# Sparse attention and a feed-forward block on one core: the products with the end keys in 64x32 tiles

## The chip, the cores and the metric

The kernel runs on one core of a Trainium2 chip. The metric is the device time of one execution in microseconds (us); the median of three runs is compared. PE is TensorE's matmul side, PEld its weight loads, DVE is VectorE, ACT is ScalarE, POOL is GpSimd, SP is SyncE. TensorE's granted clock is given as a share of 2.4 GHz.

## What is computed

Attention over 4 batches of 8 heads, 768 positions and head size 64, followed by a feed-forward block on all 3072 tokens (512 to 2048 to 512). Only some blocks of 32 keys count for a block of 32 queries:

```python
scores = scale * np.matmul(q, k.transpose(0, 1, 3, 2))
mask = np.abs(blk_i - blk_j) <= window                    # window = 1
mask = mask | (blk_i == 0) | (blk_j == 0) | (blk_i == n_blocks - 1) | (blk_j == n_blocks - 1)
for qb in range(n_blocks):
    for kb in sampled_blocks[qb]:                         # three drawn blocks
        mask[qb * block:(qb + 1) * block, kb * block:(kb + 1) * block] = True
scores = np.where(mask, scores, -1000000000.0)
...
attn = attn / (np.sum(attn, axis=-1, keepdims=True) + 1e-09)
return np.matmul(attn, v).astype(np.float32)

h = x @ w_in
sp = np.maximum(h, 0.0) + np.log1p(np.exp(-np.abs(h)))
g = h * erf(sp)
return (g @ w_out).astype(np.float32)
```

So a block of queries inside the sequence looks at eight blocks of keys: the first and the last of the sequence (the end keys), three neighbours and three drawn ones. The first and the last block of queries look at all keys.

## The kernel before

Queries and keys lie with head size on the partitions, two heads of a pair on rows 0 to 63 and 64 to 127. Work on the scores comes in units. A unit of kind "m" is four blocks of queries (128 rows of scores) of two pairs of heads; there are 10 for each batch, 40 in all. A unit "e" is the last two inner blocks of two pairs (2 for each batch, 8 in all), a unit "f" is the two end blocks of queries of one pair against all keys (4 for each batch).

`scores` (L575) makes the products of a unit in fp32, in one PSUM tile `s` of two banks (one for each head of a pair). For "m" and "e" it runs over `turns`, the two pairs: first the end keys, 64 columns (`blocks_of(rows, pr, 0, NB, NB - 1)` takes the first and the last block), into columns 192 to 255 of each group, then the six near and drawn blocks, 192 columns, for each block `j` of queries apart. The end keys are the same for all blocks of queries, so one product has all of a unit's queries of a head as its stationary operand: 64 rows by 128 columns for "m" (four products), 64 by 64 for "e" (four products). The near products have 32 stationary columns, since each block of queries has its own keys: 64 by 32 tiles, 16 products for "m" and 8 for "e". An fp32 product appears in the trace as two MATMUL and two LDWEIGHTS instructions, a product of fp16 as one of each.

`soft_max`, `soft_exp` and `soft_low` (DVE and ACT) turn `s` into probabilities in two fp16 halves, `soft_turn` transposes them by a DMA of SP's queue (on PE for the first four units), and `values` (L623) multiplies them with the rows of values two units later: 96 fp16 products of 128 by 32 tiles and 64 or 65 columns into `po` for an ordinary place (192 LDWEIGHTS and MATMUL in all), and 192 products for the places of the "e" and "f" units.

The order is written out by hand; every instruction stays in program order on its engine. After a prologue (load, scale and split the weights, four units) a loop over 96 groups of the feed-forward block runs. One step of it issues on PE, in this order: `ff_first` (24 products of 256 columns into `h`), `values` of a unit begun two units earlier, `scores` of a new unit, `ff_second` of the group before the last (12 products of 512 columns into `o`). Steps without a unit have `h` and `o` alone. The table `until` says how many units have begun by which group. `s` is one buffer, so that `scores` waits until ACT has read the unit before.

Of the kernel before, what the change touches and what calls it, by code (L numbers as in the profile page):

```python
# [19 lines left out]
BLOCK = 32  # L20
# [22 lines left out]
def sparse_attention_moe(ctx: ExitStack, tc: tile.TileContext, qT, kT, v, sampled, w_in, w_out, out):  # L43
# [22 lines left out]
    pe, act, dve, pool, sp = (InOrder(e) for e in (nc.tensor, nc.scalar, nc.vector, nc.gpsimd, nc.sync))  # L66
    B, H, D, S = qT.shape
    NB = S // BLOCK
# [38 lines left out]
    def key_blocks(b):  # L107
        return keys[:, b % 2 * (NB + 1) : (b % 2 + 1) * (NB + 1)]
# [456 lines left out]
    def near_keys(b, i, rows, pr):  # L565

        c = slice(pr * BLOCK, (pr + 1) * BLOCK)
        first = b % 2 * (NB + 1) + i - 1
        near = keys[rows, first : first + NR, c]
        apart = (kgs[b, i] - first) * HP * BLOCK  # L570
        return bass.AP(near.tensor, near.offset, [near.ap[0], (apart, 2), near.ap[1], near.ap[2]])
# [3 lines left out]
    def scores(unit):  # L575
        kind, b, n = unit[0], unit[1], unit[2:]
        tag = "_".join(str(x) for x in unit)
        s = ps_s.tile([P, 1024], F32, tag="s", name=f"s_{tag}")
        q = qts[b, n[0] if kind == "m" else MT]
        both = [slice(a * D, (a + 1) * D) for a in range(2)]  # L580

        def blocks_of(rows, pr, start, stop, step=1):
            return key_blocks(b)[rows, start:stop:step, pr * BLOCK : (pr + 1) * BLOCK]

        if kind == "f":
            (pr,) = n
            for c, e in ((0, 512), (512, S)):
                for rows in both:
                    k = blocks_of(rows, pr, c // BLOCK, e // BLOCK)
                    pe.matmul(s[rows, c:e], q[rows, pr, 2 * BLOCK :], k, start=True, stop=True)  # L590
            softs[unit] = (s[:, :S], 1, S)
            return
        if kind == "m":
            t, quad = n
            s4 = s.rearrange("p (a r w) -> p a r w", a=2, r=2)
            first, count, turns = 1 + 4 * t, 4, [(r, 0, s4[:, :, r]) for r in range(2)]
            softs[unit] = (s, 4, 256)
        else:
            (quad,) = n
            s3 = s.rearrange("p (a w) -> p a w", a=2)[:, :, :256]  # L600
            first, count, turns = NB - 3, 2, [(r, r * D, s3) for r in range(2)]
            softs[unit] = (s3, 2, 256)
        for r, o, out in turns:
            pr = 2 * quad + r
            for a, rows in enumerate(both):
                k = blocks_of(rows, pr, 0, NB, NB - 1)
                pe.matmul(
                    out[o : o + count * BLOCK, a, 192:], q[rows, pr, : count * BLOCK], k, start=True, stop=True
                )
        for r, o, out in turns:  # L610
            pr = 2 * quad + r
            for j in range(count):
                c = j * BLOCK
                for a, rows in enumerate(both):
                    place = out[o + c : o + c + BLOCK, a, :192]
                    near = near_keys(b, first + j, rows, pr)
                    pe.matmul(place, q[rows, pr, c : c + BLOCK], near, start=True, stop=True)
# [243 lines left out]
    def seen(unit):  # L861

        if unit[0] == "m":
            return unit[1:]
        if unit[0] == "f" and unit[2] % 2 == 1:
            return unit[1], MT, unit[2] // 2
        return None
# [48 lines left out]
    for quad in range(2):  # L916
        square_v(0, quad)
    scale_v(0)
    scores(units[0])
    split_v(0, 0, 0)  # L920
    split_v(0, 0, 1)
# [7 lines left out]
    have_v.add(0)  # L929

    scores(units[1])
    used_keys(units[1])
    gathers(0)
# [8 lines left out]

    soft_turn(units[1])
    scores(units[2])
    work("Di4 Qi4 Di5")
    soft_max(units[2])
# [43 lines left out]
    for m in range(len(groups) + FF_LAG):  # L990
# [12 lines left out]
        place = seen(old) if old and begun - PV_LAG >= FIRST else None  # L1003
# [82 lines left out]
```

## Time and profile before

| | us |
|---|---|
| median of 3 runs (826.76 to 829.26) | 828.74 |
| the profiled execution | 831.7 |
| its span on the core | 829.9 |
| PE busy | 698.5 |
| DVE busy | 570.1 |
| ACT busy | 551.3 |
| POOL busy | 126.8 |

The span is the time from the first to the last instruction of the profiled execution; 1.8 us of the profiled time lie around it. PE is busy for 84% of the span and the other engines for less. The first quarter is the prologue, in which PE is idle for half of the time; from then on it is busy nearly throughout. The timeline gives for each run of like instructions the start, the length, the engine, the tiles, the number of instructions, and in brackets the idle time ahead of it and what ended it. "Issue" there is a wait for nothing that the profile shows.

### The profile page before, as it was taken

How to read it: one execution, taken by the hardware profiler on the slowest of the kernel's cores; microseconds unless marked ns; L12 is line 12 of the kernel's file. 1: busy time of each engine (PE TensorE's matmuls, PEld its weight loads, DVE VectorE, ACT ScalarE, POOL GpSimd, SP SyncE). 2: the span in 40 equal slices, each digit the busy share in tenths (PEclk: the TensorE clock that was granted, in tenths of full speed). 3: DMA queues.
4: the chain of work that ended last, by engine and by line, in shares of the span. 5: the costliest groups of instructions: out<-in, count | busy, mean ns of one | idle time of the engine just before them, and what ended most of it. 6: DMA issues, size and time to landing. Idle time of an engine off the chain costs nothing. (4 is left out here: it accounts for less than half of the span.)

```text
span 829.9 us, 26567 instructions
## 1 busy us (share of the span) xinstructions
PE 698.5 (84%) x10844; PEld 460.2 (55%) x10844; DVE 570.1 (69%) x987; ACT 551.3 (66%) x943; POOL 126.8 (15%) x343
## 2 busy tenths in 40 slices
PE   1254546888986879999999988999999999999997
PEld 1133423555654647566666556666666665666664
DVE  3994696787865666885668766876677767754454
ACT  4654567987755656776668657767677676675774
POOL 4621131002222121100103231000111110000000
PEclk9999767999998999999999999999999999999999
DMA  8999963887799898773598898752688858220000
GB/s 306 289 267 295 250 164 66 164 182 196 176 197 199 215 207 185 162 167 47 134 206 193 171 223 201 177 96 45 162 192 175 182 103 184 44 53 16 1 26 26
DMA packets 199930, 131.59 MB, mean 159 GB/s; under 512 B 144000, under 2 KB 167168, under 8 KB 199808
## 3 DMA queue, kind: packets, MB, share of 16 engines
q1 hardware_dynamic: 196384, 118.10, 62.5%
q0 software_dynamic: 3424, 11.80, 4.4%
q8 instruction: 85, 1.39, 0.7%
q14 instruction: 37, 0.30, 0.1%
HBM read 83.88 MB, written 12.95 MB: 117 GB/s over the span
## 5 line engine op out<-in xcount | busy, mean ns | idle before, releaser
L59 PE MATMUL h<-xT,wi 128*128 128x256 f16 x2304 | 275.7, 277 | 17.0 <-ACT wi L59 9.3
L59 PE MATMUL o<-wo,g 128*128 128x512 f16 x1152 | 271.4, 385 | 10.1 <-issue 3.5
L59 PEld LDWEIGHTS <-wi 128*128 128x128 f16 x2304 | 227.9, 99 | 68.7 <-ACT wi L59 10.8
L59 PEld LDWEIGHTS <-g 128*128 128x128 f16 x1152 | 109.0, 99 | 150.9 <-issue 32.4
L59 ACT ACTIVATE x<-x 128x512 f32<-128x512 f32 x288 | 181.5, 630 | 9.1
L59 POOL COPY keys<-keys 128x128 f32 x264 | 92.4, 397 | 260.1 <-PE s_m L59 173.8
L59 DVE SCALAR_TENSOR_TENSOR q<-x,q 128x512 f32<-128x512 f32 x96 | 67.8, 706 | 65.4 <-ACT x L59 65.4
L59 ACT ACTIVATE x<-h,isg 128x512 f32<-128x512 f32 x96 | 65.5, 682 | 67.7 <-PE h L59 67.6
L59 ACT ACTIVATE pf_m<-s_m,nb_m 128x256 f32<-128x256 f32 x160 | 62.6, 473 | 57.1 <-DVE nb_m L59 54.2
L59 PE MATMUL s_m<-keys,qt 64*32 64x192 f32 (+1 forms) x1600 | 71.6, 344 | 12.5 <-issue 6.1
L59 ACT ACTIVATE q<-q 128x512 f32<-128x512 f32 x96 | 60.7, 633 | 32.0 <-DVE q L59 32.0
L59 DVE SCALAR_TENSOR_TENSOR q<-q,h 128x512 f32<-128x512 f32 x96 | 65.5, 683 | 22.6 <-ACT q L59 22.6
L59 DVE SCALAR_TENSOR_TENSOR g<-q,g 128x512 f16<-128x512 f32 x96 | 66.6, 694 | 3.3
L59 PE MATMUL po<-vb,pT_m 128*32 128x65 f16 (+1 forms) x3840 | 45.8, 203 | 26.9 <-DMA vb<-vtab 15.1
L59 ACT ACTIVATE q<-x 128x512 f32<-128x512 f32 x96 | 60.5, 630 | 3.0
L59 DVE TENSOR_REDUCE mx_m<-s_m 128x4 f32<-128x1024 f32 x40 | 48.8, 1219 | 19.3 <-PE s_m L59 19.0
L59 PEld LDWEIGHTS <-pT_m 128*32 128x32 f16 x3840 | 39.0, 99 | 38.5 <-DMA vb<-vtab 16.8
L59 PEld LDWEIGHTS s_m<-keys,qt 64*32 64x32 f32 (+1 forms) x1600 | 45.2, 130 | 26.4 <-issue 9.5
L59 DVE TENSOR_TENSOR p_m<-pf_m,p_m 128x1024 f16<-128x1024 f32 x40 | 49.1, 1227 | 3.2 <-ACT p_m L59 2.2
L59 DVE TENSOR_TENSOR x<-xf,x 128x512 f16<-128x512 f32 x24 | 17.6, 734 | 38.9 <-ACT x L59 38.9
L59 DVE TENSOR_SCALAR g<-q 128x512 f16<-128x512 f32 x96 | 41.6, 433 | 3.3
L59 POOL COPY keys<-wi 128x768 f32<-128x768 f32 (+1 forms) x24 | 16.3, 705 | 163.7 <-DMA wi<-in_kT_dram 163.7
(111 smaller groups left out, 523.4 us busy)
## 6 DMA issues: line engine op xcount, KB each, us to landing
vb<-vtab SPq DMA_DIRECT2D x280, 65.0 KB, 3.3
vb<-vtab SPq DMA_DIRECT2D x32, 390.0 KB, 5.0
vraw<-in_v_dram SPq DMA_DIRECT2D x10, 768.0 KB, 5.6
vtab<-vn SPq DMA_DIRECT2D x16, 390.0 KB, 5.6
vb<-vtab SPq DMA_DIRECT2D x12, 520.0 KB, 6.1
qt<-in_qT_dram SPq DMA_DIRECT2D x20, 256.0 KB, 3.5
out_dram<-wo SPq DMA_DIRECT2D x20, 256.0 KB, 5.4
vb<-vtab SPq DMA_DIRECT2D x36, 130.0 KB, 3.3
```

What stands on the lines that cost most here:

```text
L59: done = call(*args, **kwargs)
```

## The change

The end keys are multiplied for each block of queries apart, as the near keys are. For each pair the products now run over `j` and the two heads: 32 stationary columns in place of 128 ("m") or 64 ("e"), 64 moving columns as before, and the result goes to the same places. A unit "m" has 16 products with the end keys in place of 4, a unit "e" 8 in place of 4. Nothing else is changed.

```diff
@@ -602,11 +602,12 @@
             softs[unit] = (s3, 2, 256)
         for r, o, out in turns:
             pr = 2 * quad + r
-            for a, rows in enumerate(both):
-                k = blocks_of(rows, pr, 0, NB, NB - 1)
-                pe.matmul(
-                    out[o : o + count * BLOCK, a, 192:], q[rows, pr, : count * BLOCK], k, start=True, stop=True
-                )
+            for j in range(count):
+                c = j * BLOCK
+                for a, rows in enumerate(both):
+                    place = out[o + c : o + c + BLOCK, a, 192:]
+                    ends = blocks_of(rows, pr, 0, NB, NB - 1)
+                    pe.matmul(place, q[rows, pr, c : c + BLOCK], ends, start=True, stop=True)
         for r, o, out in turns:
             pr = 2 * quad + r
             for j in range(count):
```

On PE, with no other row changed there, the place of the unit of batch 3, turn 1, quad 0, between the last rows of `values` and the first of `ff_second`. Before:

```order
L59 MATMUL po_0_0_10169<-vb,pT_m_0_0_9784 32x65
L59 MATMUL s_m_1_0_10290<-keys,qt_1_9684 128x64 x4
L59 MATMUL s_m_1_0_10290<-keys,qt_1_9684 32x192 x16
L59 LDWEIGHTS g_1_2_10096
L59 MATMUL o_1_0_0_9824<-wo,g_1_2_10096 128x512
```

After:

```order
L59 MATMUL po_0_0_10577<-vb,pT_m_0_0_10180 32x65
L59 MATMUL s_m_1_0_10698<-keys,qt_1_10068 32x64 x16
L59 MATMUL s_m_1_0_10698<-keys,qt_1_10068 32x192 x16
L59 LDWEIGHTS g_1_2_10504
L59 MATMUL o_1_0_0_10220<-wo,g_1_2_10504 128x512
```

The four products with 128 stationary columns have become sixteen with 32, ahead of the sixteen near ones, and the rows around them stand where they stood. A product of fp32 is one row here with its weight load, so 16 of the trace's instructions have become 64.

The same on PE for the second "e" unit of batch 2, between the values of the end blocks and the feed-forward block. Before:

```order
L59 MATMUL po_5_0_9324<-vb,pT_f_1_9224 32x65
L59 MATMUL s_e_1_9517<-keys,qt_5_8190 64x64 x4
L59 MATMUL s_e_1_9517<-keys,qt_5_8190 32x192 x8
L59 LDWEIGHTS g_0_4_9264
L59 MATMUL o_0_0_0_9066<-wo,g_0_4_9264 128x512
```

After:

```order
L59 MATMUL po_5_0_9704<-vb,pT_f_1_9604 32x65
L59 MATMUL s_e_1_9897<-keys,qt_5_8542 32x64 x8
L59 MATMUL s_e_1_9897<-keys,qt_5_8542 32x192 x8
L59 LDWEIGHTS g_0_4_9644
L59 MATMUL o_0_0_0_9446<-wo,g_0_4_9644 128x512
```

Here four products with 64 stationary columns have become eight with 32, that is 16 of the trace's instructions have become 32.

## Rows read from the trace of the kernel before

**Rows 1.** The page: busy time with its share, and PE and its clock in 40 slices.
```profile
PE 698.5 (84%) x10844; PEld 460.2 (55%) x10844; DVE 570.1 (69%) x987; ACT 551.3 (66%) x943; POOL 126.8 (15%) x343
PE   1254546888986879999999988999999999999997
PEclk9999767999998999999999999999999999999999
```

**Rows 2.** Busy us and instructions by window: PE, PEld, DVE, ACT, POOL, clock, DMA, GB/s.
```profile
500.00:600.00 100.00, 96.80 (x1502) 62.75 (x1501) 72.33 (x131) 68.37 (x119) 9.42 (x31) 0.98 0.59 136
600.00:700.00 100.00, 97.78 (x1702) 66.60 (x1701) 75.62 (x136) 71.37 (x128) 12.31 (x42) 1.00 0.81 172
```

**Rows 3.** Timeline of PE, one step and a half: start, length, work, idle before.
```profile
642.06 1.47 PE L59 MATMUL s_m<-keys,qt 64*128 64x64 f32 x40
643.47 2.76 PE L59 MATMUL o<-wo,g 128*128 128x512 f16 x12
646.07 2.78 PE L59 MATMUL h<-xT,wi 128*128 128x256 f16 x24
648.78 0.96 PE L59 MATMUL po<-vb,pT_m 128*32 128x65 f16 x96
649.67 1.11 PE L59 MATMUL s_m<-keys,qt 64*128 64x64 f32 x15
651.17 0.86 PE L59 MATMUL s_m<-keys,qt 64*32 64x192 f32 x25 [0.39 <-issue]
```

**Rows 4.** Windows on the scores' tiles: end and near part ("m"), end part ("e").
```profile
331.28:331.87 0.59, 0.59 (x8) 0.52 (x8) 0.00 (x0) 0.00 (x0) 1.00 0.77 223
331.87:332.68 0.81, 0.81 (x34) 0.49 (x32) 0.00 (x0) 0.00 (x0) 1.00 0.37 39
...
553.94:554.22 0.28, 0.28 (x9) 0.21 (x9) 0.00 (x0) 0.00 (x0) 1.00 0.25 59
```

**Rows 5.** Groups by form, PE, all units "m": count, busy us, mean ns, idle before.
```profile
L59 PE MATMUL s_m<-keys,qt 64*32 64x192 f32 x1280 | 45.4, 354 | 5.9 <-issue 3.7 <-POOL keys L59 1.9 <-POOL vn L59 0.2
...
L59 PE MATMUL s_m<-keys,qt 64*128 64x64 f32 x320 | 29.0, 303 | 6.7 <-ACT pf_m L59 4.3 <-issue 2.4
```

**Rows 6.** Windows from one stall of PE's issue to the next, columns as in Rows 2.
```profile
206.09:231.71 25.62, 23.85 (x383) 14.95 (x383) 20.76 (x35) 19.18 (x34) 5.66 (x15) 0.93 0.74 156
231.71:252.53 20.82, 16.90 (x381) 11.61 (x380) 14.28 (x26) 10.29 (x21) 5.95 (x14) 1.00 0.97 222
...
305.80:376.61 70.81, 67.64 (x1019) 43.94 (x1020) 53.54 (x97) 51.08 (x89) 9.03 (x28) 0.98 0.82 177
...
651.16:758.86 107.69, 104.44 (x1531) 68.98 (x1530) 72.07 (x130) 74.11 (x124) 5.47 (x18) 1.00 0.46 95
```

**Rows 7.** Timeline of PE at two of these stalls.
```profile
252.53 1.25 PE L59 MATMUL s_m<-keys,qt 64*128 64x64 f32 x36 [2.39 <-issue]
...
588.11 0.88 PE L59 MATMUL s_m<-keys,qt 64*32 64x192 f32 x30 [0.82 <-issue]
```

**Rows 8.** DMA queues: packets, MB, share of 16 engines.
```profile
q8 instruction: 85, 1.39, 0.7%
```

**Rows 9.** Windows of 256 instructions that end at a stall, columns as in Rows 2.
```profile
373.43:376.61 3.18, 1.71 (x149) 1.59 (x142) 0.69 (x1) 3.05 (x5) 0.00 (x0) 1.00 1.22 99
...
584.65:588.11 3.45, 2.64 (x148) 2.14 (x133) 1.51 (x5) 2.57 (x5) 0.00 (x0) 1.00 0.26 67
755.10:758.86 3.76, 2.26 (x153) 1.71 (x139) 2.33 (x6) 2.88 (x6) 0.00 (x0) 1.00 0.01 4
```

**Rows 10.** Timeline of PE: long waits for other engines and transfers.
```profile
262.63 0.22 PE L59 MATMUL po<-vb,pT_m 128*32 128x65 f16 x1 [3.40 <-DMA vb<-vtab]
...
479.17 1.09 PE L59 MATMUL po<-vb,pT_m 128*32 128x65 f16 x96 [1.91 <-DMA pT_m<-p_m]
...
517.06 2.44 PE L59 MATMUL s_f<-keys,qt 64*64 64x512 f32 x8 [1.95 <-ACT pf_m L59]
...
692.52 1.10 PE L59 MATMUL po<-vb,pT_m 128*32 128x65 f16 x96 [1.69 <-DMA pT_m<-p_m]
```

## The prediction

> **What bounds the kernel now.** I read the page's busy lines first, then the windows, then the timeline of PE step by step. PE is the busiest engine, and from the second quarter on its slices stand at 8 and 9 tenths at the full clock [rows 1]. Late in the span it is busy for 97 to 98 us of each 100, DVE and ACT for 68 to 76 [rows 2]. The page's chain of waits ends after 3% of the span and decides nothing here. In the timeline a step runs `s`, `o`, `h`, `po`, `s` without a gap: 1.47, 2.76, 2.78 and 0.96 us [rows 3]. So in such a stretch what PE saves shortens the step.
>
> Two things break that. PE waits for transfers and for ACT in places: 3.40 us, 1.91 us, 1.95 us and 1.69 us are long ones [rows 10]. What PE saves just ahead of one of these mostly makes the wait longer. The last that does not hang on a place close by in PE's own work is at 517 us; the one at 692 us waits for a transposed unit that PE itself made earlier, so I let it move along.
>
> And PE stops where nothing holds it but "issue". Look at the counts between such stops: 383 + 383, 381 + 380, 1019 + 1020, 1531 + 1530 matmuls and weight loads [rows 6], that is 766, 761, 2039 and 3061, each a few short of 768, 768, 2048 and 3072. The few are semaphore instructions, which these counts leave out. So the stops stand at multiples of 256 instructions. The queue named "instruction" carried 85 packets of 1.39 MB in all [rows 8], 16.4 KB each; 10844 + 10844 instructions [rows 1] in 85 portions are 255 each. PE's instructions therefore come in blocks of 256, and PE stops when a block is not there yet. Two of these stops show 2.39 and 0.82 us of idle time [rows 7].
>
> How long a block takes can be read too: 256 instructions that end at a stop took 3.18, 3.45 and 3.76 us [rows 9], all in dense work that alone would be done in 1.5 to 2 us. I take 3.5 us from entering a block until the next one can be used. A block of `o` and `h` work is far longer: 48 instructions of `h` take 2.78 us and 24 of `o` 2.76 us [rows 3]. Only `po` and `s` run dense enough to outrun the supply: `po` has 192 instructions in 0.89 us, from 648.78 to 649.67 [rows 3], 4.6 ns each.
>
> **What the change saves on PE.** The end part of a unit "m" takes 0.59 us, the near part 0.81 us [rows 4]. In the end part eight weight loads of 128 columns fill 0.52 us [rows 4]; the loads set its pace. The changed end part has the form of the near one, with 64 moving columns in place of 192 and as many instructions (the near part: 1280 matmuls in 40 units [rows 5], 32 for each). By columns it takes a third of 0.81, 0.27 us; by the pace of `po`, 32 pairs of load and matmul at 9.3 ns, 0.30 us. The two ends are close, and the change of form between the parts goes away, which speaks for less. I take 0.27 and keep 0.20 to 0.30: 0.32 us saved (0.29 to 0.39). For "e" the end part takes 0.28 us [rows 4] and will have half the instructions of "m", 0.14: 0.14 saved. Were all of it to count, 40 x 0.32 + 8 x 0.14 = 13.9 us. Up to some 215 us PE is idle for much of the time [rows 1], so I count nothing there; up to 517 us the waits of rows 10 take most back. Behind 517 us stand ten units "m" and four "e": 10 x 0.32 + 4 x 0.14 = 3.8 us.
>
> The Trainium skill, "TensorE: Matmul & The Clock Gate", section "Wait — 56ns, not 53.3ns?", says that matmuls never start closer than about 25 ns. By it 32 of them would take 0.8 us, and the end part would be 0.2 us longer. The 4.6 ns for each instruction of `po` [rows 3] speaks against it.
>
> **What the change adds.** Each "m" gets 48 more instructions on PE and each "e" 16: 40 x 48 + 8 x 16 = 2048, eight more blocks. Ahead of a unit's scores stand 192 instructions of `po`; with the 80 of the scores they were 272 in some 2.0 us, now 320 in about 1.6 us. A block that begins in the first third of `po` now ends inside the scores; before, only one that began in the first 16 instructions did. I counted the changed order forward in blocks of 256, from the place that the stops of before give (a block begins 194 instructions behind PE's first), which I take as unchanged because nothing ahead of the first matmul changes. Worked in full: one block behind 517 us holds the last 166 of a `po`, the 64 of the end part and 25 near ones (and a semaphore); 166 x 4.6 ns + 0.13 (the gap between `po` and `s`) + 0.27 + 0.25 = 1.4 us against 3.5, a stop of 2.1 us. Price and contents of the others behind 517 us: 256 of the longer `po` of the end units twice (about 1.4 us: 2.1 each, or 1.5 where the block begins early in `po`, when PE's queue runs ahead), the same block as the worked one two units later (2.0), one of 120 `po`, 128 scores and 7 `o` (2.6 us: 0.9), one of 256 `po` that begins right behind `h` (0.5 to 2.1). That is six, 7.9 to 11.2 us; I take 9.3. Two more begin 20 instructions before the end of `h` and last 2.4 us; before, such a block cost 0.39 us of idle time in one place [rows 3], so 0 to 1.1 each, and I take none. The stop at 759 us ends a block that holds the same instructions before and after, and cancels.
>
> Taken away are the stops of before in this stretch. With the pace lost around them they cost 1.1 us at 588 us, 0.7 at 651 and about 0.5 elsewhere, 2.3 us [rows 3, 7]. Added: 9.3 - 2.3 = 7.0 us (5.6 to 11.1).
>
> Ahead of 517 us the same count gives about 3 us more of stops than before, and 6.6 us less of PE's work; both stand between long waits [rows 10], and I put them at nothing, between -4 and +3. No other engine's instructions change. What covers the rest: DVE and ACT have a quarter of each 100 us free [rows 2], so a step 0.3 us shorter leaves them time. More stops also give the other engines time, so some of the 7.0 is taken back from waits; I keep that in the range.
>
> Sum: 831.7 - 3.8 + 7.0 = 834.9 for the profiled execution, which stands 3.0 above the median; for the median 828.74 + 3.2, rounded 832.0.
>
> **The rivals.**
> 1. The blocks come in time, or their stops only fill waits that are there anyway, and the shorter scores count: 828.74 - 3.8 = 825; with all 30 "m" and 6 "e" behind 215 us, 10.4 us, 818. For it: most blocks of before came in time. Against: [rows 6, 7]. The Trainium skill, "Runtime: NRT & Kernel Launch", section "Instruction fetch mechanics", says that instructions come in blocks of 16 KiB, 256 of them, and that crossing into one is mostly hidden. By that rule the added instructions cost nothing, which is this rival; the block size agrees with the trace, the hiding does not.
> 2. Gain and stops cancel: half of the 7.0 us is taken back by waits, 828.74 - 3.8 + 3.5, about 828.5. For it: a stop of 2.39 us at 252 us [rows 7] stands ten us ahead of a wait for a transfer of 3.40 us [rows 10], which without the stop would have been longer.
> 3. All added stops are paid, those ahead of 517 us too, and the two uncertain ones: 828.74 - 3.8 + 11.1 + 2.2 = 838. It decides from the point at which transfers delay the blocks beyond 3.5 us.
> 4. Small products don't run at the pace of `po`: 0.2 us more for each of 40 units, 8 us: 837.
>
> **How the numbers follow.** The forecast, slower through missing instructions, has 0.50 (829.5 to 836; a fifth of it lies under 831.2), rival 1 0.24 (of this 0.05 near 818), rival 2 0.18, rival 3 0.05, rival 4 0.03. 0.3%, about what a measurement of this kernel can tell from no change, is 2.5 us. Faster by more: 0.22, from rival 1. Within: rival 2, a fifth of the forecast, and 0.04 from the edges of rival 1 and of the forecast, 0.32. Slower: what is left, 0.46. The range leaves out the far end of rival 1 and most of rival 3: 822 to 837. The likeliest case alone spans 829.5 to 836.
>
> **What would show it.** The end part of an undisturbed unit at about 0.27 us and no gap before the near part; 32 matmuls in its form; 93 packets on the instruction queue; stops of issue at multiples of 256 instructions, at least a dozen of them, several inside `s` right behind `po` and inside the long `po` of the end units. It would be wrong if the stops stand where they stood, or if fewer appear because the blocks begin elsewhere; then PE's step is simply shorter, and rival 1 holds.

## The result and the profile after

The changed kernel takes 838.42 us, the median of ten runs (833.09 to 840.43); the kernel before, run beside it ten times, 827.89 (825.23 to 834.43). The ratio over all runs is 1.0111, between 1.0081 and 1.0141: 9.2 us slower, 6.7 to 11.7 (the two medians alone lie 10.5 us apart). The forecast was 832.0 and the range ended at 837. The direction was right, the size was not.

The profiled execution took 838.55 us, its span 836.8. The page, with the lines that answer to [rows 1] and [rows 8]:

```profile
PE 694.4 (83%) x11868; PEld 455.9 (54%) x11868; DVE 567.9 (68%) x987; ACT 551.3 (66%) x943; POOL 128.9 (15%) x343
PE   1242735888987989998899898999899999999997
PEclk9995666999998999999999999999999999999999
q8 instruction: 93, 1.52, 0.8%
```

PE is busy for 4.1 us less than before and the span is 6.9 us longer, so PE stands idle for 11 us more. 1024 matmuls and 1024 weight loads are added, and eight packets of instructions, 93 in place of 85.

The timeline of PE at an undisturbed step (start, length, work, count, idle time before), to set beside [rows 3]:

```profile
637.08 0.96 PE L59 MATMUL po<-vb,pT_m 128*32 128x65 f16 x96
637.97 1.26 PE L59 MATMUL s_m<-keys,qt 64*32 64x64 f32 x64
639.16 2.76 PE L59 MATMUL o<-wo,g 128*128 128x512 f16 x12
641.76 2.78 PE L59 MATMUL h<-xT,wi 128*128 128x256 f16 x24
```

The scores take 1.26 us in place of 1.47. The end part alone, from the windows on the scores' tiles, for a unit "m" and a unit "e", to set beside [rows 4]:

```profile
399.80:400.07 0.27, 0.27 (x33) 0.27 (x33) 0.00 (x0) 0.00 (x0) 1.00 0.00 1
...
561.52:561.66 0.14, 0.14 (x17) 0.14 (x25) 0.00 (x0) 0.00 (x0) 1.00 0.00 0
```

0.27 and 0.14 us, as forecast. But the end part became 0.32 us shorter and the scores only 0.21: the near part now fills 1.26 - 0.27 = 0.99 us where 1.47 - 0.59 = 0.88 were left before.

The stops of PE's issue, windows from one to the next as in [rows 6], and two blocks of 256 that end at one as in [rows 9]:

```profile
594.93:604.30 9.37, 8.73 (x254) 6.06 (x255) 6.35 (x11) 4.94 (x10) 3.37 (x12) 1.00 0.66 153
604.30:619.82 15.52, 14.20 (x255) 9.44 (x255) 12.10 (x23) 10.38 (x19) 1.78 (x6) 1.00 0.87 184
...
591.62:594.93 3.31, 1.63 (x145) 1.50 (x137) 0.99 (x2) 2.81 (x5) 0.00 (x0) 1.00 0.26 70
615.87:619.82 3.95, 2.63 (x153) 1.77 (x137) 3.78 (x9) 3.42 (x6) 1.78 (x6) 1.00 1.01 236
```

509 and 510 instructions lie between these stops, a few short of 512, and the blocks take 3.3 and 4.0 us: the mechanism of the prediction. What it did to the time is read from the view of waits, cut by stretch: who waited for what, us in total, times, longest. First the kernel before, up to 215 us, from there to 570 us, and behind:

```profile
PE po L59 <- issue: 6.1, 3, 2.9
...
PE s_m L59 <- issue: 4.9, 3, 2.4
PE o L59 <- issue: 3.5, 2, 2.6
PE po L59 <- issue: 3.2, 2, 1.7
...
PE s_m L59 <- issue: 1.2, 2, 0.8
```

The kernel after, in the same three stretches:

```profile
PE po L59 <- issue: 8.5, 3, 4.9
...
PE s_m L59 <- issue: 15.6, 8, 2.9
PE po L59 <- issue: 3.8, 2, 3.0
PE o L59 <- issue: 1.1, 1, 1.1
PE s_e L59 <- issue: 0.2, 1, 0.2
...
PE po L59 <- issue: 1.7, 1, 1.7
PE o L59 <- issue: 1.3, 1, 1.3
PE s_m L59 <- issue: 1.2, 2, 0.6
```

6.1, 11.6 and 1.2 us became 8.5, 20.7 and 4.2: 14.5 us more, 33.4 in place of 18.9, and 11.5 of them stand ahead of 570 us, 10.5 of these ahead of 517 us, in the stretch that the prediction had put at nothing. Most wait in front of a piece of `s`, eight times in the middle stretch.

The stops are not all of it. `o`, unchanged in the code, on the page of the kernel before and of the kernel after (count, busy time, mean in ns, idle time before):

```profile
L59 PE MATMUL o<-wo,g 128*128 128x512 f16 x1152 | 271.4, 385 | 10.1 <-issue 3.5
L59 PE MATMUL o<-wo,g 128*128 128x512 f16 x1152 | 277.1, 391 | 8.0 <-issue 2.5
```

`o` takes 5.7 us more. As PE's busy time as a whole fell by 4.1 us, its other work takes 9.8 us less, about the 9.5 that 40 x 0.21 and 8 x 0.14 us of shorter scores make. PE's idle time other than the stops fell from 112.5 to 109.0 us. So in the two profiled executions 14.5 us of stops and 5.7 of slower `o`, less 9.8 of shorter work and 3.5 of shorter waits, make the 6.9 us by which the span grew. Nearly all of it is there at 523 us; the same `h` before and after:

```profile
522.74 2.78 PE L59 MATMUL h<-xT,wi 128*128 128x256 f16 x24
529.42 2.78 PE L59 MATMUL h<-xT,wi 128*128 128x256 f16 x24
```

### The profile page after: what moved, and what is told of

It is laid out like the page before. It is cut to its first block, busy times and chain, and to the rows that moved or that the text cites. A ratio compares the mean times of both kernels' runs of the same rounds, so it can differ in the third digit from the quotient of the medians.

```text
span 836.8 us, 28615 instructions
## 1 busy us (share of the span) xinstructions
PE 694.4 (83%) x11868; PEld 455.9 (54%) x11868; DVE 567.9 (68%) x987; ACT 551.3 (66%) x943; POOL 128.9 (15%) x343
## 5 line engine op out<-in xcount | busy, mean ns | idle before, releaser
L59 PE MATMUL o<-wo,g 128*128 128x512 f16 x1152 | 277.1, 391 | 8.0 <-issue 2.5
L59 PEld LDWEIGHTS <-wi 128*128 128x128 f16 x2304 | 227.8, 99 | 66.9 <-ACT wi L59 11.5
L59 POOL COPY keys<-keys 128x128 f32 x264 | 95.2, 409 | 262.6 <-PE s_m L59 173.2
L59 PE MATMUL s_m<-keys,qt 64*32 64x192 f32 (+1 forms) x2560 | 63.7, 297 | 23.8 <-issue 16.8
L59 PEld LDWEIGHTS s_m<-keys,qt 64*32 64x32 f32 x2560 | 39.8, 112 | 34.3 <-issue 21.0
```

The lines of the kernel that those rows point to most:

```text
L59: done = call(*args, **kwargs)
```

## The experiments

Each kernel was timed beside the kernel before, whose median was 828 to 830 us in every group; ratios are to it.

**Instructions without the saving, the saving without instructions.** First the kernel before with as many instructions as the changed one, the added ones as one-column products behind `po`:

```diff
+        for n in range(24 if t < MT else 8):
+            j = n % 4 * 32
+            pe.matmul(room[j : j + 32, 300 + n // 4 : 301 + n // 4], fill[:, j : j + 32], fill[:, :1], ...)
```

> The kernel before, with the added instructions but without the change: each `values` of an ordinary place gets 24 products of one column behind its 96 (48 instructions), each of the end blocks 8 (16 instructions), 2048 in all, as many as the change adds; they go to unused columns of the same PSUM bank and nobody reads them. Theory of the instruction supply: PE's own work grows by 40 x 0.22 us, and the stops at multiples of 256 instructions grow as in the changed kernel (some 20 of them, 30 us or more in the profile): 8 to 16 us slower than before. Rival, that the small tiles of the end products themselves cost the time (their form, their banks): only PE's own work counts, half of it hidden as elsewhere: 2 to 5 us slower, with the stops of issue as before (about 13).

846.1 us, ratio 1.0193 (1.0144 to 1.0242). In its timeline `po` and the products behind it take 1.06 us where `po` alone took 0.89 [rows 3], so 40 x 0.17 + 8 x 0.06 = 7.3 of the 16.0 us are their own work and 8.7 us are left. Its trace has two things to show for them: 24.6 us of stops in place of 18.9, and 276.0 us of `o` in place of 271.4, 10.3 us in sum, of which shorter waits for others give 2.3 back. Then the reverse, which leaves out the end products of 36 units, so that its output is not the one asked for:

```diff
+                if kind == "m" and unit not in units[:FIRST]:
+                    pe.matmul(out[o : o + BLOCK, a, :1], q[rows, pr, :BLOCK], k[:, 0, :1], start=True, stop=True)
+                    continue
...
-                    place = out[o + c : o + c + BLOCK, a, :192]
+                    place = out[o + c : o + c + BLOCK, a, : 192 + 64 * more]
```

> Left out: the end products of the 36 units m of the loop; their 64 columns are multiplied with other keys, as the last quarter of near products that are now 256 columns wide, and four one-column products stand where the end products stood. So PE has as many instructions as before, at the same places, and a step is some 0.3 us shorter, about what the changed products save. Theory (the saving is real and counts where PE bounds, what takes it is the added instructions): stops at the same places as before, 823 us, 819 to 826. Rival 1 (PE's saving counts for nothing, other engines and transfers set the pace): 830 within 2 us. Rival 2 (a shorter step reaches more waits and stops and ends slower): 833 or more.

826.93 us, ratio 0.9969 (0.9947 to 0.9991), between the 823 of the theory and the 830 of the first rival. Its scores, in the timeline of PE:

```profile
639.20 1.18 PE L59 MATMUL s_m<-keys,qt 64*32 64x1 f32 x40
```

0.29 us shorter than 1.47, in 36 units, 10.4 us of PE's work; 2.6 us arrive (0.7 to 4.4). That is 10 x 0.29 = 2.9, the ten units of the last stretch, and fits the prediction's rule that a saving counts only there. In its trace PE is busy for 9.1 us less and its idle time other than the stops is 7.0 us longer, so waits take most of it back. The saving is real, and small; by these two runs the loss of the changed kernel comes with its instructions.

**The places of the blocks.** One-column products ahead of the first scores, where PE waits anyway, move all later work against the blocks:

```diff
+    pad = ps_h.tile([P, 512], F32, tag="h", name="pad")
+    for n in range(60):
+        j = n % 4 * 32
+        pe.matmul(pad[j : j + 32, n // 4 : n // 4 + 1], unity[:, j : j + 32], unity[:, :1], start=True, stop=True)
```

With 32, 60, 96 and 128 such products (64, 120, 192 and 256 instructions) in the kernel before, and with 32 and 60 in the changed one:

> The changed kernel with 120 more instructions (60 products of one column) ahead of the first scores, where PE is idle: all blocks of 256 begin 120 instructions earlier in the program. Theory of the instruction supply: the stops stand at other places of the program, again at multiples of 256 counted from PE's first instruction; counted in the same way as for the prediction they come out some 8 us shorter in sum, and the time 1 to 4 us below the changed kernel. Rival, stops tied to a place of the program (a transfer that is late there): the same places, the same time.

> The kernel before with 60 one-column products (120 instructions) ahead of the first scores, while PE waits there anyway: all blocks begin 120 instructions earlier in the program, nothing else changes. Theory (the places of the blocks decide which stops there are): stops at other places, their number behind 215 us anywhere from 6 to 16 in place of 12, and a time that differs from that of before by up to 6 us either way, 822 to 834. Rival (the places do not matter): within 1 us of before.

> The kernel before with 32 one-column products (64 instructions) ahead of the first scores: all blocks of instructions begin 64 earlier in the program. Theory (the kernel before has its blocks at lucky places; 120 instructions ahead cost 6 us): slower than before by 2 to 9 us, 832 to 839. Rival (only some places are bad, the usual is 830): 828 to 832.

> The changed kernel with the same 64 instructions ahead. Theory (the changed kernel costs some 6 us wherever the blocks fall, since a unit's run of dense instructions grew from 272 to 320): slower than the kernel before with the same 64 ahead, by 3 to 10 us. Rival (the two differ by the places of their blocks alone): within 3 us of it or faster.

> The kernel before with 96 one-column products (192 instructions) ahead: a third place for its blocks. Theory: 832 to 839. Rival (the usual is 830): 828 to 832.

> The kernel before with 128 one-column products (256 instructions, one whole block) ahead of the first scores. The blocks of all later work begin at the same instructions as in the kernel before. Theory (with 64, 120 and 192 instructions ahead the kernel became 4, 6 and 9.5 us slower because its blocks moved to worse places): back to the time of before, 828 to 832. Rival (the products put ahead cost that time themselves, some 0.1 us each, through the start): 840 or more.

| instructions ahead | kernel before | changed kernel |
|---|---|---|
| 0 | 1 | 1.0111 (1.0081 to 1.0141) |
| 64 | 1.0061 (1.0031 to 1.0090) | 1.0137 (1.0100 to 1.0175) |
| 120 | 1.0071 (1.0047 to 1.0095) | 1.0188 (1.0143 to 1.0234) |
| 192 | 1.0117 (1.0084 to 1.0150) | |
| 256 | 1.0016 (0.9995 to 1.0038) | |

With 64 to 192 instructions ahead the kernel before loses 5 to 10 us, and with a whole block ahead it has its time back. So the products themselves cost some 1.3 us (-0.4 to 3.1), and the rest goes with where the blocks fall: the kernel before stands at a good place, by 5 us and more. The changed kernel, expected to become 1 to 4 us faster with 120 ahead, became slower too. The changed kernel is 0.8 and 1.2% slower than the kernel before with as many instructions ahead, so at three places of its blocks it loses about as much. The places explain what one number more or less may cost; they do not explain the change away.

How a moved block becomes time is not shown. It is not by longer stops: with 64, 120 and 192 instructions ahead the kernel before has 8.4, 12.6 and 20.6 us of stops in its trace, against 18.9 with none, and the changed kernel 28.0 and 19.1 with 64 and 120, against 33.4. In the two with the fewest, PE's other idle time is longer in exchange: 129.4 us in the kernel before with 64 ahead (112.5 with none), and 129.8 in the changed one with 120 (109.0). What made these waits longer was not tried.

**The first four units and the loop.** The changed form in one of the two alone; 192 instructions lie between them:

```diff
+            wide = count * BLOCK if unit in units[:FIRST] else BLOCK
```

> The changed products in all units but the first four, which keep the old form: 4 x 48 = 192 instructions fewer than the changed kernel, so every block in the loop begins at another instruction. Theory (added blocks are paid for, whichever place they fall at): the one late block of 84 us (a stop of 5.2 us, against 3.1 before) goes, the first h group begins at 100 us as before, and the loop still has some 12 to 18 stops behind 215 us; 835 us, 831 to 839, slower than before. Rival 1 (the loss is that one late block): 828 or less. Rival 2 (the changed products themselves cost the time, by the clock or by their pace): within 2 us of the changed kernel, 838.

> The changed products in the first four units alone; the loop keeps the old form and has its old number of instructions, 192 places later. Theory (late block at 84 us, plus places of the stops): the first h group begins 3 to 3.5 us later than before, the loop has the usual 8 to 14 stops at other places; 832 us, 828 to 836. Rival (only what is in the loop counts): 828 within 2 us, and the delay of the first h group is taken back by the waits before 320 us.

839.8 us, ratio 1.0112 (1.0081 to 1.0143), and 837.41, ratio 1.0088 (1.0063 to 1.0114). Both lose nearly all of it, so the two don't add up, and both end above the range expected of them. Each moves the loop's blocks by 192 instructions against the changed kernel or the one before; after the table above that alone is worth as much. These two runs tell nothing on the parts.

**Larger tiles, fewer instructions.** End products of the units "m" in 64x64 tiles:

```diff
+            wide = 2 * BLOCK
```

> The end products of a unit m in 64x64 tiles: eight products of 64 stationary columns in place of four of 128, 16 added instructions a unit in place of 48, 640 in all, two and a half blocks in place of eight; the end units are as before. Theory (instructions cost, short loads save): the end part takes 0.27 to 0.35 us in place of 0.59, and few stops are added; 828 us, 824 to 832, level with before or faster. Rival (any small tile costs, whatever its number of instructions): 833 to 838.

835.95 us, ratio 1.0059 (1.0036 to 1.0081). A step of PE at this kernel's scores:

```profile
647.28 1.27 PE L59 MATMUL s_m<-keys,qt 64*64 64x64 f32 x48
```

1.27 us against 1.26: the same saving with a third of the added instructions, and about half the loss. The expectation of 828 was missed: 640 instructions are two and a half blocks, so the later work stands at other places too, and how much of the loss is places this run can't tell.

**Orders without a dense run.** If `po` and `s` don't stand together, no block lies within them. Two orders were run, each with the old and with the changed form. In the first `po` comes behind `o`, and the gathers and the normalization move along:

```diff
-        if place:
-            values_of(place)
-        if steps:
-            gathers(begun)
...
+        if place:
+            values_of(place, range(2, 4) if split else range(4))
+        if steps:
+            gathers(begun)
```

> The kernel before with another order on PE: `values` comes behind `ff_second` in place of ahead of `scores` (with its norm and the gathers behind it), and the long `values` of the end blocks is cut in two halves, one ahead of `scores` and one behind `ff_second`. No instruction is added; the dense `po` and `s` no longer stand side by side, so 256 instructions hold at least 24 of `o` or 48 of `h` and last 3.5 us or more. Theory of the instruction supply: nearly no stops of issue in the loop, and 3 to 7 us faster than before, unless the later `po` brings waits of its own. Rival, stops of issue are not about density (the DMA queue is late at those moments): as many stops as before, time within 2 us or slower by what the later `po` costs.

> The changed kernel in the same other order as e4_spread_before. Theory of the instruction supply: with the dense stretches apart the added instructions cost nothing, and what is left of the change is 0.21 us less of PE's work for each unit m (read from the step times of the changed kernel), part of it taken back by waits: 1 to 5 us faster than e4_spread_before, so the change turns from a loss into a small gain. Rival, the small tiles cost the time: still 8 to 11 us slower than e4_spread_before.

In the second `po` comes ahead of `h`, and the orders on the queues stay:

```diff
+        if place:
+            values_of(place)
         if group:
             ff_first(*group)
             ff_logs(*group)
-        if place:
-            values_of(place)
```

> The kernel before with po ahead of h in every step of the loop: PE runs po, h, s, o in place of h, po, s, o, so that the 192 dense instructions of po and the 80 of s never stand together and no block fits in one dense run; the queues' orders and the number of instructions stay. Theory (stops behind the middle of the span are paid in full): the stops of s behind po go, at most 5 are left behind 215 us in place of 10, and the time falls by 2 to 5 us: 826, 823 to 829. Rival (waits take the place of the stops, as in the order tried first): 832 to 836.

> The changed kernel with the same order, po, h, s, o. Theory (the change loses by the stops that its longer dense run brings; without them its shorter scores count): at most 6 stops behind 215 us in place of 16, 824, 820 to 829, level with the same order of the kernel before or up to 5 us under it. Rival (the changed products cost time of their own, or a faster step only runs into waits): 5 to 14 us slower than the same order of the kernel before, 832 to 843.

First order, old form: 834.68 us, ratio 1.0073 (1.0038 to 1.0108); changed form: 848.38, 1.0236 (1.0191 to 1.0281). Second order, old form: 839.78, 1.0140 (1.0098 to 1.0182); changed form: 846.6, 1.0217 (1.0179 to 1.0255). All four are slower than the kernel before, and all four missed what was expected. From the waits of the second order, the old form and then the changed one:

```profile
PE po L59 <- DMA pT_m<-p_m: 29.9, 9, 11.8
...
PE s_m L59 <- issue: 1.6, 1, 1.6
```

```profile
PE po L59 <- DMA pT_m<-p_m: 36.4, 10, 10.5
...
PE s_m L59 <- issue: 7.1, 4, 2.6
```

The second order takes most stops away from `s` (before 6.1 us, after 16.8 in the whole span); of all stops it leaves 14.8 us of 18.9 in the old form and 23.4 of 33.4 in the changed one. But `po` now asks for the transposes an `h` earlier and waits 29.9 and 36.4 us for them, where the kernel before waited 6.4. The rival of these expectations held in kind: waits take the place of the stops. And the changed form is slower than the old one by 6.8 us in the second order and by 13.7 in the first. In the first, the changed form still has 10.8 us of stops against 3.1 in the old form, 7.7 of the 13.7, and its trace shows 11.5 us more of PE's other idle time; why is open. These 10.8 us are fewer than the 18.9 of the kernel before, which is some 19 us faster: in this order it is not the stops alone that carry the loss.

**By stretch.** The units of one batch add 10 x 48 + 2 x 16 = 512 instructions, two whole blocks. So one batch can be changed, and the others keep their places:

```diff
+            wide = BLOCK if b in (1, 2) else count * BLOCK
```

and the same for batch 3 and for batch 0.

> The changed products in the 20 units m and four units e of batches 1 and 2 alone (221 to 565 us). They add 20 x 48 + 4 x 16 = 1024 instructions, four whole blocks, so ahead of them and behind them the blocks stand at the same instructions as in the kernel before. The prediction put nearly all of this stretch at nothing: 828, within 3 us of before. Theory now (added stops are paid there too, the 20 shorter units give some 4 us back): 10 or more stops between 215 and 570 us in place of 8, and 833, 831 to 837.

> The changed products in batch 3 alone (572 us to the end): 512 instructions more, two whole blocks; everything ahead of 572 us is as before. This is the stretch from which the prediction took its whole change. By its sum 831; theory now (four stops more, 4 us, less 10 x 0.21 + 2 x 0.16 = 2.4 us of saving): 829 to 831. Rival (the last stretch carries the whole loss): 834 or more.

> The changed products in batch 0 alone (up to 207 us): 512 instructions more, two whole blocks; everything behind is as before. The prediction put it at nothing, since PE is idle for much of this stretch. Theory now (the block at 84 us comes late, the first h group begins 3 us later, and the waits between 260 and 320 us take most of it back): 829, 827 to 831. Rival (the start carries the loss): 833 or more.

| changed | stretch | us | ratio | more than before, us |
|---|---|---|---|---|
| batch 0 | to 207 us | 833.36 | 1.0053 (1.0029 to 1.0077) | 4.4 |
| batches 1 and 2 | 221 to 565 us | 833.40 | 1.0060 (1.0031 to 1.0090) | 5.0 |
| batch 3 | 572 us to the end | 829.67 | 1.0016 (0.9993 to 1.0039) | 1.3 |

4.4 + 5.0 + 1.3 = 10.7 us, within the changed kernel's 6.7 to 11.7: the parts add up, though each is known to some 2.5 us either way. Batch 0 was expected at 829 and took what its rival said, 833; the other two came as expected. The waits of the kernel with batches 1 and 2 changed, from 215 to 570 us and behind:

```profile
PE s_m L59 <- issue: 16.4, 8, 3.3
PE po L59 <- issue: 3.1, 2, 2.7
...
PE s_m L59 <- issue: 1.2, 2, 0.9
```

Here the middle has the stops of the changed kernel, 19.5 us in place of 11.6, and the stretch behind it those of the kernel before, 1.2 us in two. 7.9 us of stops more, less 20 x 0.21 + 4 x 0.14 = 4.8 us of shorter scores, are 3.1 us; measured were 5.0 (2.6 to 7.5). The page of this run shows that the sum lacks two terms:

```profile
L59 PE MATMUL o<-wo,g 128*128 128x512 f16 x1152 | 279.5, 394 | 9.4 <-DVE g L59 4.1
```

In its profiled execution the span is 3.7 us longer than before: 7.0 us more of stops in the whole span and 8.1 of slower `o`, less 4.9 of other work and 6.5 of other waits. Here nearly all of the stops were taken back by waits, and it is `o` that is left.

Where `o` is slower can be seen in the timeline right behind a stop, and in the windows there (columns as in [rows 2]), of the changed kernel:

```profile
379.67 0.21 PE L59 MATMUL po<-vb,pT_e 128*32 128x64 f16 x2 [3.02 <-issue]
...
380.84 4.45 PE L59 MATMUL o<-wo,g 128*128 128x512 f16 x12
...
462.72 1.20 PE L59 MATMUL s_m<-keys,qt 64*32 64x192 f32 x29 [2.31 <-issue]
463.86 4.07 PE L59 MATMUL o<-wo,g 128*128 128x512 f16 x12
```

```profile
379.70:381.10 1.40, 1.40 (x69) 0.92 (x69) 0.69 (x4) 0.00 (x0) 0.02 (x1) 1.00 0.04 12
381.20:384.60 3.40, 3.40 (x10) 1.21 (x8) 2.95 (x6) 1.36 (x3) 1.89 (x6) 0.50 0.00 0
384.70:388.00 3.30, 3.30 (x29) 2.66 (x28) 1.25 (x3) 0.05 (x1) 0.00 (x0) 1.00 0.41 79
```

An `o` that takes 2.76 us elsewhere takes 4.45 and 4.07 here. PE stopped for 3.02 us, worked for 1.5 us at 2.4 GHz, and then the granted clock is 0.50, the level of 1.2 GHz, from 381.2 to 384.6 us, and 1.00 again after that. So a long stop can cost its length and 1.3 to 1.7 us more. Not each does: behind one of 2.61 us, at 415 us in the kernel with batches 1 and 2 changed, `o` took 2.76. That the stop brings the lower clock is read from where the two stand; no run tried it apart. No kernel of these runs that computes all of the output was faster than the kernel before.

## Why the prediction was wrong

**What bounds, and the blocks: right.** 93 packets, end part 0.27 us, stops at multiples of 256 instructions, inside `s` behind `po`, more than a dozen: all as written. The Trainium skill, "Runtime: NRT & Kernel Launch", section "Instruction fetch mechanics", says that the crossing into a block is mostly hidden. The added 14.5 us of stops speak against it for code as dense as `po` and `s`.

**The saving: mis-sized by a third.** 0.32 us a unit was expected and 0.21 came, because the near part grew by 0.11 [rows 3, 4]. Behind 517 us that makes 10 x 0.21 + 4 x 0.14 = 2.7 us in place of 3.8. That it counts there and hardly elsewhere is borne out by the run with as many instructions as before.

**The last stretch: right within its error.** Behind 517 us the sum said 3.2 us slower. The trace shows 3.9 us of stops more (to the 4.2 behind 570 us come 0.7 and 0.2 from 517 to 570, against 1.2 before) where 7.0 were put, less 2.7 of saving; behind the `h` at 522.74 us the two executions differ by 0.2 us. The run with batch 3 alone gave 1.3 us, -0.6 to 3.2. The mechanism held and the stops were put too high: those worked out at up to 2.1 us lasted 0.2 to 1.7.

**The step that failed: "Ahead of 517 us ... I put them at nothing, between -4 and +3."** Batches 0 to 2 cost 9.4 us there. Three things were wrong in it. The count: about 3 us more of stops were expected ahead of 517 us, and 10.5 came (before 6.1 + 11.6, after 8.5 + 19.7). The cover: the waits of [rows 10] were to swallow the stops as they swallow a saving. In the changed kernel PE's other waits shrank by 3.5 us against 14.5 of stops; with batches 1 and 2 alone changed they shrank by 6.5 against 7.0. So the waits swallow a part, and how much was not settled. And a term that the sum does not have: work behind a stop at the lower clock. `o` took 5.7 us more in the changed kernel, 8.1 with batches 1 and 2 changed, and 4.6 in the run with the added instructions and the old scores.

The measured 838.42 is the number of the third rival, all added stops are paid, 838 us, to which the prediction gave 0.05. What it says is near; that its number fits is luck. Its 11.1 us already hold the two uncertain stops, 11.2 - 2.3 + 2.2, which the sum then adds a second time (without them it gives 836), and it has no term for the stops ahead of 517 us, where most of them came. The prediction should have priced a stop apart from a saving, with the clock behind it, and not taken from the long waits that it is free.

**One stop that no rule foretold.** At 83.77 us PE waited 4.95 us for a block, and the first `h` came 3.5 us later than before; in the kernel with batch 0 alone 3.85 us at 81.59. In the changed kernel:

```profile
77.00 1.82 PE L59 MATMUL po<-vb,pT_m 128*32 128x65 f16 x92 [0.61 <-DMA vb<-vtab]
83.77 0.21 PE L59 MATMUL po<-vb,pT_m 128*32 128x65 f16 x1 [4.95 <-issue]
```

From 65.2 to 81.4 us no packet of instructions moved there, while the other queues did; in the kernel before one did in the same stretch. The queues of the changed kernel there, then of the kernel before:

```profile
q1 hardware_dynamic: 1280, 3.15, 67.3%
q0 software_dynamic: 485, 1.72, 32.5%
```

```profile
q1 hardware_dynamic: 1214, 2.85, 61.0%
q0 software_dynamic: 532, 1.92, 33.9%
q8 instruction: 1, 0.02, 0.5%
```

Why the packet waited is open. So is where batch 0 loses its 4.4 us: its profiled execution took 830.6 us, less than its median, and shows 9.2 us of stops up to 215 us against 6.1, but no lasting delay behind 260 us.

## What to carry to other kernels

Count instructions as a cost beside time where an engine runs dense: here 2048 more cost 9 us over what they saved, and 64x64 tiles shortened the scores as much with a third of them. That a saving ahead of a long wait is worthless doesn't make a stop there free; price the two apart, and look at the clock behind the stop. And before a difference of one per cent is believed, move the code by part of a block and by a whole one: here that alone was worth up to 10 us, and the kernel before stood at a good place.

## What was not expected of the hardware

A stop of 2 to 3 us for instructions can be followed by a stretch at half the clock, in which one `o` took 4.45 us in place of 2.76; over the whole span `o` lost 5.7 us. No packet of instructions moved for 16 us once, from 65.2 to 81.4 us, and PE stood still for 4.95 us. And the near part, unchanged in the code, took 0.99 us in place of 0.88 behind the new end part; its cause was not tried.
